# Loading q and k by eights of heads, 14 tokens to a partition

## Chip, cores and metric

One core of one Trainium2 chip. The time is the device time of one execution in microseconds (us). A ratio is the mean time of one kernel's fast runs over the mean of the other's fast runs of the same rounds, so it is not quite the ratio of the medians quoted beside it.

## The reference

Attention with normalized q and k over (8 batches, 12 heads, 448 tokens, 64 features), then a soft mixture of experts over the 3584 tokens with their 768 features.

```python
q_n, k_n = rmsnorm(q, g_q), rmsnorm(k, g_k)               # over the 64 features
attn = softmax(q_n @ k_n^T / 8);  x = attn @ v             # -> x (3584, 768)
logits = x @ phi                                          # (3584, 32), 8 experts x 4 slots
slot_input = softmax(logits, axis=0).T @ x                # (32, 768)
slot_out[e] = relu(slot_input[e] @ w1[e]) @ w2[e]         # w1 (768, 1024), w2 (1024, 768)
out = softmax(logits, axis=1) @ slot_out
```

q, k and v are 11 MB each in float32; the weights are 50 MB, stored in SBUF as bf16.

## The kernel before

It works through 24 groups of four heads (a "Q"). ACT or POOL squares the raw q and k, DVE sums, ACT makes the inverse root, POOL scales to bf16, PE transposes, DVE evacuates; then PE makes scores, ACT exponentials, PE the products with v. (PE is the matrix engine TensorE, ACT the scalar, DVE the vector and POOL the general-purpose engine.) The engine SP issues the loads of q, k and v and the stores; POOL issues the weights, one by one, after the Qs listed in `WQ`. All loads of q and k go through one function, those of v through another:

```python
def load(Q, t):                                # one transfer, 128 partitions x 2 runs of 1792 bytes
    src = (q, k)[t][Q // QB, Q % QB * 4:Q % QB * 4 + 4].rearrange("h t d -> (h t) d")
    nc.sync.dma_start(out=raw(Q, t), in_=src.rearrange("(r p s) d -> p r (s d)", r=2, s=NT))

def loadv(Q):                                  # four transfers into 64 partitions, runs of 1024 or 768 bytes
    for r in range(2):
        src = v[...].rearrange("h (p s) d -> p h (s d)", s=NT)
        m = (4 - r) * D
        nc.sync.dma_start(out=vraw(Q)[0:64, :, 4 * D * r:4 * D * r + m], in_=src[:, :, :m])
        nc.sync.dma_start(out=vraw(Q)[64:128, :, 3 * D * r:3 * D * r + NT * D - m], in_=src[:, :, m:])
# ... cut ...
WQ = [0, 2, 4, 7, 9, 12, 14, 16, 18, 20, 21, 21, 22, NQ, NQ]     # after which Q each weight is issued
```

So SP issues 2 + 4 transfers per Q, 12 per eight heads. The built program gives these transfers eight completion semaphores in turn: the trace shows eight numbers on SP's 161 transfers. From the ninth on, 150 of 153 raise the same semaphore as the eighth before them; none of the 153 is issued before that one has landed, and 34 are issued within 0.1 us of its landing.

The softmax here doesn't subtract the row's maximum and nothing guards it: scores larger than these inputs give would overflow.

Of the kernel before, what the change touches and what calls it, by code (L numbers as in the profile page):

```python
# [18 lines left out]
def kernel(  # L19
# [14 lines left out]
    assert (B, H, S, D) == (8, 12, 448, 64)  # L34
    NT = 7
# [10 lines left out]
    NPRE = 10  # L46
# [18 lines left out]
    def place(name, elems, n):  # L65
        off = sum(sizes)
        sizes.append(elems * n)
        places[name] = (off, elems, n)

    place("rawq", 2 * 2 * NT * D, 4)  # L70
    place("rawk", 2 * 2 * NT * D, 3)
    place("sq", 2 * 2 * 2 * NT * D, 1)
    place("qkn", 2 * NT * 128, 1)
    place("vraw", 2 * 2 * NT * D, 2)
    place("vext", 2 * 8 * (D + 1), 2)
    place("kT", 2 * S, 2)
    place("qT", 2 * S, 2)
    place("x", 4 * 4 * D, 4)
    place("xT", DC * 128, 4)
    place("attn", 2 * S, 7)  # L80
    arena = big.tile([128, sum(sizes)], BF16, tag="arena", name="arena")

    def at(name, i):
        off, elems, n = places[name]
        off += (i % n) * elems
        return arena[:, off:off + elems]
# [10 lines left out]
    wplace += [arena[:, i * WSZ:(i + 1) * WSZ] for i in range(4)]  # L97
    wplace += [arena[:, sum(sizes) - WSZ:], wplace[0]]
# [6 lines left out]
    def raw(Q, t):  # L105
        return at(("rawq", "rawk")[t], Q).bitcast(F32).rearrange("p (r x) -> p r x", r=2)

    def load(Q, t):
        src = (q, k)[t][Q // QB, Q % QB * 4:Q % QB * 4 + 4].rearrange("h t d -> (h t) d")
        nc.sync.dma_start(out=raw(Q, t), in_=src.rearrange("(r p s) d -> p r (s d)", r=2, s=NT))  # L110

    def vraw(Q):
        return at("vraw", Q).bitcast(F32).rearrange("p (w x) -> p w x", w=2)

    def loadv(Q):


        for r in range(2):
            src = v[Q // QB, Q % QB * 4 + 2 * r:Q % QB * 4 + 2 * r + 2].rearrange("h (p s) d -> p h (s d)", s=NT)
            m = (4 - r) * D  # L120
            nc.sync.dma_start(out=vraw(Q)[0:64, :, 4 * D * r:4 * D * r + m], in_=src[:, :, :m])
            nc.sync.dma_start(out=vraw(Q)[64:128, :, 3 * D * r:3 * D * r + NT * D - m], in_=src[:, :, m:])
# [8 lines left out]
    load(0, 0)  # L131
    load(0, 1)
# [4 lines left out]
    for Q in (1, 2):  # L137
        load(Q, 0)
        load(Q, 1)
    loadv(0)  # L140
    load(3, 0)
# [11 lines left out]
    def kT(Q):  # L153
        return at("kT", Q).rearrange("p (w c) -> p w c", w=2)

    def qT(Q):
        return at("qT", Q).rearrange("p (w c) -> p w c", w=2)
# [12 lines left out]
    def sq(t):  # L170
        return at("sq", 0).bitcast(F32).rearrange("p (t x) -> p t x", t=2)[:, t]

    def square(Q, t, pool=False):

        r = raw(Q, t).rearrange("p r x -> p (r x)")
        if pool:
            nc.gpsimd.tensor_tensor(sq(t), r, r, op=MUL)  # L177
        else:
            nc.scalar.activation(out=sq(t), in_=r, func=ACTF.Square)  # L179

    def rowsum(Q, t):

        n = Q + t
        if n not in sss:
            sss[n] = small.tile([128, 2, 2 * NT], F32, tag="ss", name="ss")
            rss[n] = small.tile([128, 2, 2 * NT], F32, tag="rs", name="rs")
        nc.vector.reduce_sum(sss[n][:, t], sq(t).rearrange("p (r d) -> p r d", d=D), axis=AX)  # L187
# [23 lines left out]
    def trans(Q, t):  # L211


        order = range(NT) if t == 0 else (0, 4, 1, 5, 2, 6, 3)
        pts[t] = psum.tile([128, NT, 128], BF16, tag="misc", name="qkTp")
        for i, s in enumerate(order):
            nc.tensor.transpose(pts[t][:, i], qkn(Q, t)[:, s], ident)  # L217

    def evac(Q, t):
        pt = pts.pop(t).rearrange("p s (w c) -> p w s c", w=2)  # L220
        if t == 0:
            nc.vector.tensor_scalar(qT(Q).rearrange("p w (s c) -> p w s c", s=NT), pt, gg, None, op0=MUL)  # L222
        else:
            nc.vector.tensor_copy(kT(Q).rearrange("p w (s c) -> p w s c", s=NT), pt)  # L224
# [31 lines left out]
    def xq(Q):  # L256
        return at("x", Q).rearrange("p (c n) -> p c n", c=4)

    def norm(Q, w, half):
        o = ovs.pop(half)[:, :, :2 * D + 2].rearrange("p c (h n) -> p c h n", h=2)  # L260
        rd = small.tile([128, 2, 2, 1], F32, tag="rd", name="rd")
        nc.vector.reciprocal(rd, o[:, :, :, D:])  # L262
        nc.vector.tensor_tensor(xq(Q).rearrange("p c (h w d) -> p c h w d", h=2, w=2)[:, 2 * half:2 * half + 2, :, w],  # L263
                                o[:, :, :, :D], rd.to_broadcast([128, 2, 2, D]), op=MUL)

    def xT(dc, n=1):
        off = places["xT"][0] + dc * 512
        return arena[:, off:off + n * 512].rearrange("p (c t) -> p c t", t=128)
# [7 lines left out]
    def moe_evac(Q):  # L276
        nc.vector.tensor_copy(xT(Q % QB * 2, 2), xps.pop(Q))  # L277
# [10 lines left out]
    def moe_sin(b):  # L288
# [17 lines left out]
        nc.vector.tensor_copy(eT[r, :, b % 2], ep[r].rearrange("n (s p) -> n s p", s=NT))  # L306


    square(0, 0)
    rowsum(0, 0)  # L310
    square(0, 1)
    rowsum(0, 1)
# [5 lines left out]
    trans(0, 1)  # L318
    square(1, 0)
# [3 lines left out]
    nc.vector.tensor_mul(gg, g2[:, 0:1], g2[:, 1:2])  # L323
    evac(0, 0)
    evac(0, 1)
    square(1, 1)
    rowsum(1, 1)
    square(2, 0)
    vcopy(0)

    WQ = [0, 2, 4, 7, 9, 12, 14, 16, 18, 20, 21, 21, 22, NQ, NQ]

    for Q in range(NQ + 2):
        on, ahead = Q < NQ, Q + 2 < NQ
        moe = Q - 2 if 0 <= Q - 2 < NQ else None
        mb = moe // QB if moe is not None and moe % QB == QB - 1 else None
        if Q == 0:
            load(4, 0)
            load(3, 1)
        elif Q + 4 < NQ:  # L340
            load(Q + 4, 1)
            if Q + 5 < NQ:
                load(Q + 5, 0)
# [3 lines left out]
        if Q == 0:  # L347
            rowsum(2, 0)
        else:
            if Q + 3 < NQ:  # L350
                square(Q + 3, 0)
            if ahead:
                square(Q + 2, 1, True)
        if 0 <= Q - 1 < NQ:
            norm(Q - 1, 0, 1)
        if Q + 1 < NQ and Q:
            for t in range(2):
                trans(Q + 1, t)
                evac(Q + 1, t)
        if ahead and Q:  # L360
            scaleqk(Q + 2, 0)
# [3 lines left out]
        if Q == 0:  # L365
            square(2, 1)
            rowsum(2, 1)
        if 0 <= Q - 1 < NQ:
            ov(Q - 1, 1, 0)
# [6 lines left out]
        if Q == 0:  # L376
            rsqrt(2)
            scaleqk(1, 1)
            trans(1, 0)
            evac(1, 0)  # L380
            scaleqk(2, 0)
            square(3, 0)
            rowsum(3, 0)
        elif Q + 3 < NQ:
            rowsum(Q + 3, 0)
# [9 lines left out]
        if ahead and Q:  # L395
            rowsum(Q + 2, 1)
        if Q == 0:
            loadv(2)
            load(5, 0)
            load(4, 1)  # L400
            loadv(3)
        elif Q + 3 < NQ:
            loadv(Q + 3)
# [3 lines left out]
        if Q == 0:  # L407
            trans(1, 1)
            evac(1, 1)
        if 0 <= Q - 1 < NQ:  # L410
            moe_x(Q - 1)
        if ahead:
            rsqrt(Q + 3, 0 if Q + 3 < NQ else 1)
            scaleqk(Q + 2, 1)
# [4 lines left out]
        if 0 <= Q - 1 < NQ:  # L419
            moe_evac(Q - 1)  # L420
        if mb is not None:
            moe_sin(mb)
# [120 lines left out]
```

## Time and profile before

| | before |
|---|---|
| time, median (range of 3 runs) | 282.89 us (282.38 to 288.27) |
| first and last attention exponential on ACT | 13.3 and 208.8 us |
| after the last exponential (experts, output) | 73.5 us |
| mean traffic of the 16 DMA engines | 247 GB/s |
| mean granted TensorE clock (share of full speed) | 0.836 |

The lines of the page, of the chain and of the DMA views are shown in the prediction. In this trace q1 has 2576 packets of 4 bytes for SP's 161 transfers, 16 each. They are read here as one completion for every DMA engine that a transfer ran on, so that the count "under 512 B" tells on how many engines the transfers ran. That is an inference; the packets in flight in the changed kernel, 4 at once for 89% of a stretch where the count says 4, agree with it (see "Which engines").

### The profile page before, as it was taken

To read this page: it belongs to the slowest core of one execution; us is meant where nothing else is said; L and a number is where in the kernel's file an instruction comes from. 1 tells how busy PE (TensorE), PEld (TensorE's weight loads), DVE (VectorE), ACT (ScalarE), POOL (GpSimd) and SP (SyncE) were. 2 spreads that over 40 slices of the span, in tenths; PEclk is the share of its full clock that TensorE was granted. 3 is DMA by queue.
4 is the path that set the end of the run, shared out by engine and by line. 5 is a ranking of instruction groups with operands and counts; after the bars stand their busy time and mean duration, and the time that the engine had idled before them with its cause. 6 is when DMAs were issued, how large, how long until landed. Compare 5 with 4: busy or idle time off the path is not lost.

```text
span 282.3 us, 8543 instructions
## 1 busy us (share of the span) xinstructions
PE 224.2 (79%) x3588; PEld 148.7 (53%) x3588; DVE 175.5 (62%) x381; ACT 191.8 (68%) x270; POOL 169.6 (60%) x189
## 2 busy tenths in 40 slices
PE   7568888998599999999989978988978655788800
PEld 3234554755365576566556545655657645743300
DVE  3756777888268889879878865866563101148800
ACT  4798999899379989998998967878850000036600
POOL 0779999994869998999999966788322000000000
PEclk9859999999789999999999995999996555555555
DMA  6999999999999999999999999969999999528997
GB/s 188 303 256 256 256 265 244 268 254 264 237 246 252 270 262 244 277 235 255 274 254 264 238 261 247 251 145 206 201 208 212 212 211 210 104 94 356 412 412 290
DMA packets 45079, 69.82 MB, mean 247 GB/s; under 512 B 3952, under 2 KB 36720, under 8 KB 45040
## 3 DMA queue, kind: packets, MB, share of 16 engines
q1 hardware_dynamic: 29328, 44.05, 53.2%
q0 software_dynamic: 15392, 25.22, 49.2%
q8 instruction: 28, 0.46, 0.6%
q14 instruction: 11, 0.09, 0.1%
q10 hardware_dynamic: 320, 0.00, 0.1%
HBM read 83.46 MB, written 11.01 MB: 335 GB/s over the span
## 4 chain that ended last, share of the span: by engine, by line
PE 31%; DMA 27%; POOL 16%; ACT 8%; issue 7%; DVE 4%; SPq 0%; POOLq 0%; ACTq 0%
DMA arena<-in_v_dram 19%; POOL arena L199 11%; DMA arena<-in_q_dram 9%; PE ov L253 6%; ACT arena L242 5%; PE sc L241 4%; PE hTp L463 4%; PE op L503 4%; PE soTp L473 4%; PE qkTp L217 3%; PE op L504 2%; POOL arena L207 2%; PE sinp L294 1%; DVE ss L187 1%; PE lg L283 1%
## 5 line engine op out<-in xcount | busy, mean ns | idle before, releaser
L242 ACT ACTIVATE arena<-sc 128x896 bf16<-128x896 f32 x168 | 144.6, 916 | 12.9 <-PE sc L241 10.1
L199 POOL TENSOR_TENSOR arena<-arena,rs 128x896 bf16<-128x896 f32 x48 | 82.2, 1715 | 17.4 <-ACT rs L192 15.9
L253 PE MATMUL ov<-arena 128*128 128x65 bf16 (+1 forms) x1344 | 64.9, 201 | 0.2 <-ACT arena L242 0.2
L253 PEld LDWEIGHTS <-arena 128*128 128x128 bf16 x1344 | 50.6, 99 | 20.0 <-issue 19.7
L241 PE MATMUL sc<-arena 64*128 64x448 bf16 x288 | 54.3, 373 | 7.4 <-ACT arena L242 6.6
L187 DVE TENSOR_REDUCE ss<-arena 128x14 f32<-128x896 f32 x48 | 51.6, 1077 | 8.4 <-ACT arena L179 8.4
L263 DVE TENSOR_TENSOR arena<-ov,rd 128x256 bf16<-128x256 f32 x96 | 40.8, 425 | 3.3
L507 ACT ACTIVATE wown<-op,arena 128x768 f32<-128x768 f32 x14 | 12.4, 900 | 42.5 <-PE op L504 42.5
L217 PE MATMUL qkTp<-ident,arena 128*128 128x128 bf16 x336 | 27.1, 226 | 16.2 <-POOL arena L199 15.5
L177 POOL TENSOR_TENSOR arena<-arena 128x896 f32<-128x896 f32 x21 | 35.4, 1688 | 0.2
L179 ACT ACTIVATE arena<-arena 128x896 f32<-128x896 f32 x27 | 25.6, 951 | 11.3 <-DMA arena<-in_q_dram 9.7
L217 PEld LDWEIGHTS <-arena 128*128 128x128 bf16 x336 | 19.7, 100 | 24.8 <-POOL arena L199 20.1
L241 PEld LDWEIGHTS <-arena 64*128 64x128 bf16 x288 | 16.6, 93 | 25.6 <-issue 13.8
L262 DVE RECIPROCAL rd<-ov 128x4 f32<-128x4 f32 x96 | 17.1, 178 | 12.9 <-PE ov L253 12.4
L224 DVE COPY arena<-qkTp 128x896 bf16<-128x896 bf16 x24 | 14.9, 622 | 11.8 <-PE qkTp L217 11.3
L222 DVE TENSOR_SCALAR arena<-qkTp,gg 128x896 bf16<-128x896 bf16 x24 | 16.4, 684 | 7.0 <-PE qkTp L217 6.7
L274 PE MATMUL xTp<-ident,arena 128*128 128x128 bf16 x192 | 18.1, 227 | 2.2 <-DVE arena L263 1.7
L277 DVE COPY arena<-xTp 128x1024 bf16<-128x1024 bf16 x24 | 16.4, 683 | 5.5 <-PE xTp L274 5.5
L207 POOL CAST arena<-arena 128x384 bf16<-128x384 f32 x24 | 12.3, 514 | 9.4 <-DMA arena<-in_v_dram 8.3
L503 PE MATMUL op<-arena,eT 32*128 32x512 bf16 x28 | 16.0, 616 | 1.4 <-ACT wown L507 0.7
L509 DVE TENSOR_SCALAR wown<-op,arena 128x768 f32<-128x768 f32 x14 | 14.2, 1017 | 4.6 <-PE op L504 4.4
L274 PEld LDWEIGHTS <-arena 128*128 128x128 bf16 x192 | 11.3, 100 | 9.9 <-DVE arena L263 5.9
(61 smaller groups left out, 204.6 us busy)
## 6 DMA issues: line engine op xcount, KB each, us to landing
wown<-in_moe_w_dram POOLq DMA_DIRECT2D x10, 1536.0 KB, 16.4
arena<-in_q_dram SPq DMA_DIRECT2D x24, 448.0 KB, 10.4
arena<-in_k_dram SPq DMA_DIRECT2D x24, 448.0 KB, 9.3
out_dram<-wown SPq DMA_DIRECT2D x11, 768.0 KB, 8.5
arena<-in_moe_w_dram POOLq DMA_DIRECT2D x5, 1536.0 KB, 19.6
arena<-in_v_dram SPq DMA_DIRECT2D x48, 128.0 KB, 8.0
arena<-in_v_dram SPq DMA_DIRECT2D x48, 96.0 KB, 8.4
out_dram<-wown SPq DMA_DIRECT2D x6, 384.0 KB, 7.1
```

The lines of the kernel that those rows point to most:

```text
L177: nc.gpsimd.tensor_tensor(sq(t), r, r, op=MUL)
L179: nc.scalar.activation(out=sq(t), in_=r, func=ACTF.Square)
L187: nc.vector.reduce_sum(sss[n][:, t], sq(t).rearrange("p (r d) -> p r d", d=D), axis=AX)
L199: (eng or nc.gpsimd).tensor_tensor(qkn(Q, t).rearrange("p s (r d) -> p s r d", r=2), raw(Q, t).rearrange("p r (s d) -> p s r d", d=D), rs. ...
L207: nc.gpsimd.tensor_copy(vext(Q)[:, :, 5:8, :D], vr[:, :, 4:7])
L217: nc.tensor.transpose(pts[t][:, i], qkn(Q, t)[:, s], ident)
L241: nc.tensor.matmul(sc[:, j, :S], kT(Q)[r, i // 4, c0:c0 + 128], qT(Q)[r, i // 4], start=True, stop=True)
L242: nc.scalar.activation(out=attn(i), in_=sc[:, :, :S], func=ACTF.Exp, scale=0.125)
L253: nc.tensor.matmul(ovs[half][:, c, o0:o0 + m], attn(i)[:, j, c0:c0 + 128], mov, start=(n == 0 and c == 0), stop=(n == 6), skip_group_check ...
L263: nc.vector.tensor_tensor(xq(Q).rearrange("p c (h w d) -> p c h w d", h=2, w=2)[:, 2 * half:2 * half + 2, :, w], o[:, :, :, :D], rd.to_bro ...
L274: nc.tensor.transpose(xps[Q][:, i], xq(Q)[:, i % 4, i // 4 * 128:i // 4 * 128 + 128], ident)
L503: nc.tensor.matmul(op[:, 0], eTtok(j, s), so4[r, :512], start=True, stop=True, tile_position=tp)
```

## The change

**Intent.** Fewer and longer packets. q and k come by eights of heads; a partition holds 14 successive tokens of a head, one run of 3584 bytes in place of two of 1792. A unit of work is then seven of the 14 tokens of all eight heads, so both units of an eight must be ready before its first Q, and everything up to the transpose moves one Q earlier. The first two Qs keep smaller loads for an early start. The larger raw buffers cost one weight its own space (nine for ten); the late weights get places that free earlier. The core of the diff:

```diff
-    NPRE = 10
+    NPRE = 9
-    def load(Q, t):
-        src = (q, k)[t][Q // QB, Q % QB * 4:Q % QB * 4 + 4].rearrange("h t d -> (h t) d")
-        nc.sync.dma_start(out=raw(Q, t), in_=src.rearrange("(r p s) d -> p r (s d)", r=2, s=NT))
+    def load(O, t):
+        src = (q, k)[t].rearrange("b h t d -> (b h) (t d)")[8 * O:8 * O + 8].rearrange("(h r) (p x) -> r h p x", r=2, p=32)
+        dst = at(("rawq", "rawk")[t], O).bitcast(F32).rearrange("p (r x) -> p r x", r=2)
+        for r in range(2):
+            nc.sync.dma_start(out=dst[:, r], in_=src[r])
+    def load4(n, t):
+        src = (q, k)[t].rearrange("b h t d -> (b h) (t d)")[4 * n:4 * n + 4].rearrange("(w r) (p a x) -> w r a p x", r=2, p=32, a=2)
+        for w in range(2):
+            for r in range(2):
+                nc.sync.dma_start(out=raw(n, t)[64 * w:64 * w + 64, r], in_=src[w, r])
     def loadv(Q):
+        src = v.rearrange("b h t d -> (b h) (t d)")[4 * Q:4 * Q + 4].rearrange("(w r) (p a x) -> r a p w x", r=2, p=32, a=2)
         for r in range(2):
-            src = v[...].rearrange("h (p s) d -> p h (s d)", s=NT)
             m = (4 - r) * D
-            (two transfers into 64 partitions)
+            for a in range(2):
+                (two transfers into 32 partitions)
-    WQ = [0, 2, 4, 7, 9, 12, 14, 16, 18, 20, 21, 21, 22, NQ, NQ]
+    WQ = [0, 2, 4, 7, 9, 11, 13, 15, 17, 18, 20, 21, 22, NQ - 1, NQ]
  ... cut: places in SBUF, evacuations by (token, half, block), the loop with units one Q earlier ...
```

More of the change, by code (lines that the diff above doesn't have):

```diff
@@ L65, in place @@
     def place(name, elems, n):
-        off = sum(sizes)
-        sizes.append(elems * n)
-        places[name] = (off, elems, n)
-    place("rawq", 2 * 2 * NT * D, 4)
-    place("rawk", 2 * 2 * NT * D, 3)
+        for _ in range(n):
+            places.setdefault(name, (elems, []))[1].append(sum(sizes))
+            sizes.append(elems)
+    for i in range(2):
+        place("rawq", 2 * 4 * NT * D, 1)
+        place("rawk", 2 * 4 * NT * D, 1)
     place("sq", 2 * 2 * 2 * NT * D, 1)
@@ L74 @@
     place("vraw", 2 * 2 * NT * D, 2)
+    for i in range(2):
+        place("kT", 4 * S, 1)
+        place("qT", 4 * S, 1)
+    place("free", 256, 1)
+    place("attn", 2 * S, 7)
     place("vext", 2 * 8 * (D + 1), 2)
-    place("kT", 2 * S, 2)
-    place("qT", 2 * S, 2)
     place("x", 4 * 4 * D, 4)
     place("xT", DC * 128, 4)
-    place("attn", 2 * S, 7)
     arena = big.tile([128, sum(sizes)], BF16, tag="arena", name="arena")
     def at(name, i):
-        off, elems, n = places[name]
-        off += (i % n) * elems
+        elems, offs = places[name]
+        off = offs[i % len(offs)]
         return arena[:, off:off + elems]
@@ L96 @@
     wplace = [wown[:, i * WSZ:(i + 1) * WSZ] for i in range(NPRE)]
-    wplace += [arena[:, i * WSZ:(i + 1) * WSZ] for i in range(4)]
-    wplace += [arena[:, sum(sizes) - WSZ:], wplace[0]]
+    wplace += [arena[:, i * WSZ:(i + 1) * WSZ] for i in range(5)]
+    o = places["attn"][1][0]
+    wplace += [arena[:, o:o + WSZ], wplace[0]]
     wview = lambda ap, i: ap.rearrange("p (c f) -> p c f", c=DC if i % 2 == 0 else FC)
@@ L103, in loadw, with raw @@
         nc.gpsimd.dma_start(out=wt[i], in_=wsrc(i))
-    def raw(Q, t):
-        return at(("rawq", "rawk")[t], Q).bitcast(F32).rearrange("p (r x) -> p r x", r=2)
-    def load(Q, t):
-        src = (q, k)[t][Q // QB, Q % QB * 4:Q % QB * 4 + 4].rearrange("h t d -> (h t) d")
-        nc.sync.dma_start(out=raw(Q, t), in_=src.rearrange("(r p s) d -> p r (s d)", r=2, s=NT))
+    def raw(n, t):
+        r = at(("rawq", "rawk")[t], n // 2).bitcast(F32)
+        if n < 2:
+            return r[:, n * 2 * NT * D:(n + 1) * 2 * NT * D].rearrange("p (r x) -> p r x", r=2)
+        return r.rearrange("p (r a x) -> p r a x", r=2, a=2)[:, :, n % 2]
+    def load(O, t):
[8 more added lines that the diff above has]
+                nc.sync.dma_start(out=raw(n, t)[64 * w:64 * w + 64, r], in_=src[w, r])
     def vraw(Q):
@@ L115, in loadv @@
     def loadv(Q):
+        src = v.rearrange("b h t d -> (b h) (t d)")[4 * Q:4 * Q + 4].rearrange("(w r) (p a x) -> r a p w x", r=2, p=32, a=2)
         for r in range(2):
-            src = v[Q // QB, Q % QB * 4 + 2 * r:Q % QB * 4 + 2 * r + 2].rearrange("h (p s) d -> p h (s d)", s=NT)
             m = (4 - r) * D
-            nc.sync.dma_start(out=vraw(Q)[0:64, :, 4 * D * r:4 * D * r + m], in_=src[:, :, :m])
-            nc.sync.dma_start(out=vraw(Q)[64:128, :, 3 * D * r:3 * D * r + NT * D - m], in_=src[:, :, m:])
+            for a in range(2):
+                nc.sync.dma_start(out=vraw(Q)[32 * a:32 * a + 32, :, 4 * D * r:4 * D * r + m], in_=src[r, a, :, :, :m])
+                nc.sync.dma_start(out=vraw(Q)[64 + 32 * a:96 + 32 * a, :, 3 * D * r:3 * D * r + NT * D - m], in_=src[r, a, :, :, m:])
     ones = const.tile([128, 128], BF16)
@@ L130 @@
         nc.tensor.matmul(warm, wone[:, :128], wone, start=True, stop=True)
-    load(0, 0)
-    load(0, 1)
+    load4(0, 0)
+    load4(0, 1)
     g2 = const.tile([128, 2], F32)
@@ L136 @@
         nc.scalar.dma_start(out=g2[half * D:(half + 1) * D, 1:2], in_=g_k.rearrange("(d o) -> d o", o=1))
-    for Q in (1, 2):
-        load(Q, 0)
-        load(Q, 1)
+    load4(1, 0)
+    load4(1, 1)
     loadv(0)
-    load(3, 0)
+    load(1, 0)
+    load(1, 1)
     loadv(1)
@@ L153, in kT @@
     def kT(Q):
-        return at("kT", Q).rearrange("p (w c) -> p w c", w=2)
+        return at("kT", Q // 2).rearrange("p (q w c) -> p q w c", q=2, w=2)[:, Q % 2]
     def qT(Q):
-        return at("qT", Q).rearrange("p (w c) -> p w c", w=2)
+        return at("qT", Q // 2).rearrange("p (q w c) -> p q w c", q=2, w=2)[:, Q % 2]
     for i in range(2):
@@ L173, in square @@
     def square(Q, t, pool=False):
-        r = raw(Q, t).rearrange("p r x -> p (r x)")
+        r, s = raw(Q, t), sq(t).rearrange("p (r x) -> p r x", r=2)
         if pool:
-            nc.gpsimd.tensor_tensor(sq(t), r, r, op=MUL)
+            nc.gpsimd.tensor_tensor(s, r, r, op=MUL)
         else:
-            nc.scalar.activation(out=sq(t), in_=r, func=ACTF.Square)
+            nc.scalar.activation(out=s, in_=r, func=ACTF.Square)
     def rowsum(Q, t):
@@ L184, in rowsum @@
         if n not in sss:
-            sss[n] = small.tile([128, 2, 2 * NT], F32, tag="ss", name="ss")
-            rss[n] = small.tile([128, 2, 2 * NT], F32, tag="rs", name="rs")
+            sss[n] = small.tile([128, 2, 2 * NT], F32, tag="ss", name="ss", bufs=3)
+            rss[n] = small.tile([128, 2, 2 * NT], F32, tag="rs", name="rs", bufs=3)
         nc.vector.reduce_sum(sss[n][:, t], sq(t).rearrange("p (r d) -> p r d", d=D), axis=AX)
@@ L219, in evac @@
     def evac(Q, t):
-        pt = pts.pop(t).rearrange("p s (w c) -> p w s c", w=2)
+        pt = pts.pop(t)
+        T = at(("qT", "kT")[t], Q // 2)
+        if Q < 2:
+            T = T.rearrange("p (q w s c) -> p q s w c", q=2, w=2, s=NT)[:, Q]
+            pt = pt.rearrange("p s (w c) -> p s w c", w=2)
+        else:
+            T = T.rearrange("p (w s a c) -> p a s w c", w=4, s=NT, a=2)[:, Q % 2]
+            pt = pt.rearrange("p s (w c) -> p s w c", w=4)
         if t == 0:
-            nc.vector.tensor_scalar(qT(Q).rearrange("p w (s c) -> p w s c", s=NT), pt, gg, None, op0=MUL)
+            nc.vector.tensor_scalar(T, pt, gg, None, op0=MUL)
         else:
-            nc.vector.tensor_copy(kT(Q).rearrange("p w (s c) -> p w s c", s=NT), pt)
+            nc.vector.tensor_copy(T, pt)
     def attn(i):
@@ L262, in norm @@
         nc.vector.reciprocal(rd, o[:, :, :, D:])
-        nc.vector.tensor_tensor(xq(Q).rearrange("p c (h w d) -> p c h w d", h=2, w=2)[:, 2 * half:2 * half + 2, :, w],
+        nc.vector.tensor_tensor(xq(Q).rearrange("p c (w h d) -> p c h w d", h=2, w=2)[:, 2 * half:2 * half + 2, :, w],
                                 o[:, :, :, :D], rd.to_broadcast([128, 2, 2, D]), op=MUL)
     def xT(dc, n=1):
-        off = places["xT"][0] + dc * 512
+        off = places["xT"][1][0] + dc * 512
         return arena[:, off:off + n * 512].rearrange("p (c t) -> p c t", t=128)
@@ L305, in moe_sin @@
                                 tile_position=(lo, b // 2 * NS))
-        nc.vector.tensor_copy(eT[r, :, b % 2], ep[r].rearrange("n (s p) -> n s p", s=NT))
-    square(0, 0)
-    rowsum(0, 0)
-    square(0, 1)
-    rowsum(0, 1)
+        nc.vector.tensor_copy(eT[r, :, b % 2].rearrange("n s (p a) -> n s a p", a=2),
+                              ep[r].rearrange("n (s a p) -> n s a p", s=NT, a=2))
+    for t in range(2):
+        square(0, t)
+        rowsum(0, t)
     rsqrt(0, 0, 1)
@@ L318 @@
     trans(0, 1)
+    nc.vector.tensor_mul(gg, g2[:, 0:1], g2[:, 1:2])
+    evac(0, 0)
+    evac(0, 1)
     square(1, 0)
@@ L322 @@
     scaleqk(1, 0)
-    nc.vector.tensor_mul(gg, g2[:, 0:1], g2[:, 1:2])
-    evac(0, 0)
-    evac(0, 1)
     square(1, 1)
     rowsum(1, 1)
+    rsqrt(2, 1, 2)
     square(2, 0)
     vcopy(0)
-    WQ = [0, 2, 4, 7, 9, 12, 14, 16, 18, 20, 21, 21, 22, NQ, NQ]
+    WQ = [0, 2, 4, 7, 9, 11, 13, 15, 17, 18, 20, 21, 22, NQ - 1, NQ]
     for Q in range(NQ + 2):
-        on, ahead = Q < NQ, Q + 2 < NQ
+        on = Q < NQ
         moe = Q - 2 if 0 <= Q - 2 < NQ else None
         mb = moe // QB if moe is not None and moe % QB == QB - 1 else None
-        if Q == 0:
-            load(4, 0)
-            load(3, 1)
-        elif Q + 4 < NQ:
-            load(Q + 4, 1)
-            if Q + 5 < NQ:
-                load(Q + 5, 0)
         if on:
@@ L347 @@
         if Q == 0:
+            scaleqk(1, 1, nc.vector)
+            load(2, 0)
+            load(2, 1)
             rowsum(2, 0)
-        else:
+            rsqrt(2, 0, 1)
+            square(2, 1, True)
+            trans(1, 0)
+            evac(1, 0)
+            scaleqk(2, 0)
+        elif Q == 1:
+            square(4, 0)
+        else:
+            if Q + 4 < NQ:
+                square(Q + 4, 0)
             if Q + 3 < NQ:
-                square(Q + 3, 0)
-            if ahead:
-                square(Q + 2, 1, True)
+                square(Q + 3, 1, True)
         if 0 <= Q - 1 < NQ:
             norm(Q - 1, 0, 1)
-        if Q + 1 < NQ and Q:
+        if Q + 2 < NQ and Q:
             for t in range(2):
-                trans(Q + 1, t)
-                evac(Q + 1, t)
-        if ahead and Q:
-            scaleqk(Q + 2, 0)
+                trans(Q + 2 if Q > 1 else 2, t)
+                evac(Q + 2 if Q > 1 else 2, t)
+        if Q == 1:
+            scaleqk(3, 0)
+        elif Q + 3 < NQ and Q > 1:
+            scaleqk(Q + 3, 0)
+            if Q % 2 == 0 and Q + 6 < NQ:
+                load(Q // 2 + 3, 0)
         if on:
@@ L365 @@
         if Q == 0:
-            square(2, 1)
             rowsum(2, 1)
+            square(3, 0)
+        elif Q == 1:
+            scaleqk(3, 1, nc.vector)
+            load(3, 0)
+            load(3, 1)
+            square(4, 1, True)
         if 0 <= Q - 1 < NQ:
@@ L376 @@
         if Q == 0:
-            rsqrt(2)
-            scaleqk(1, 1)
-            trans(1, 0)
-            evac(1, 0)
-            scaleqk(2, 0)
-            square(3, 0)
-            rowsum(3, 0)
-        elif Q + 3 < NQ:
-            rowsum(Q + 3, 0)
+            rsqrt(3, 1, 2)
+            trans(1, 1)
+            evac(1, 1)
+            scaleqk(2, 1)
+            rowsum(3, 0)
+            square(3, 1, True)
+        elif Q == 1:
+            rowsum(4, 0)
+            trans(3, 0)
+            evac(3, 0)
+            rsqrt(4, 0, 1)
+            scaleqk(4, 0)
+        elif Q + 4 < NQ:
+            rowsum(Q + 4, 0)
         if on:
@@ L394 @@
             norm(Q - 1, 1, 1)
-        if ahead and Q:
-            rowsum(Q + 2, 1)
         if Q == 0:
+            rowsum(3, 1)
             loadv(2)
-            load(5, 0)
-            load(4, 1)
-            loadv(3)
         elif Q + 3 < NQ:
+            rowsum(Q + 3, 1)
+        if Q + 3 < NQ:
             loadv(Q + 3)
@@ L406 @@
             score(Q, 4)
-        if Q == 0:
-            trans(1, 1)
-            evac(1, 1)
+        if Q == 1:
+            trans(3, 1)
+            evac(3, 1)
         if 0 <= Q - 1 < NQ:
             moe_x(Q - 1)
-        if ahead:
-            rsqrt(Q + 3, 0 if Q + 3 < NQ else 1)
-            scaleqk(Q + 2, 1)
+        if Q == 0:
+            rsqrt(3, 0, 1)
+            rsqrt(4, 1, 2)
+        elif Q + 3 < NQ:
+            if Q == 1:
+                rsqrt(5, 1, 2)
+                square(5, 0)
+            else:
+                rsqrt(Q + 4, 0 if Q + 4 < NQ else 1)
+            scaleqk(Q + 3, 1)
+            if Q % 2 == 0 and Q + 6 < NQ:
+                load(Q // 2 + 3, 1)
         if on:
@@ L420 @@
             moe_evac(Q - 1)
+        if Q == 1:
+            rowsum(5, 0)
+            rsqrt(5, 0, 1)
         if mb is not None:
```

## The prediction

In this text and in the expectations, k is the number of DMA engines that one transfer runs on, and a ring is the work that is queued for one engine. That k would be 4 for the loads of eight heads and 2 for load4, and that the same few engines would serve them all, no trace showed when this was written: it was the author's estimate, and the result tests it. The estimate of 393 us for the last k is the 383 of the sum plus 10 for empty stretches between loads, about 1 us for an eight, which no trace showed either.

> **What bounds the kernel now.** I read the page first (engines, slices, DMA queues), then the chain that ended last in order of time, then the DMA view over two stretches, then what the DMA-issuing queue (SP) waits for. From the page:
>
> ```profile
> span 282.3 us, 8543 instructions
> ...
> DMA  6999999999999999999999999969999999528997
> ...
> DMA packets 45079, 69.82 MB, mean 247 GB/s; under 512 B 3952, under 2 KB 36720, under 8 KB 45040
> ...
> q1 hardware_dynamic: 29328, 44.05, 53.2%
> q0 software_dynamic: 15392, 25.22, 49.2%
> ```
>
> The DMA row is 9 in nearly every slice. No compute engine is above 80% (PE 79%, ACT 68%). q1 is what SP issues (q, k, v and the output), q0 the weights, cast on the way. Together they are 102% of the 16 engines' span. But a full row alone doesn't prove that DMA sets the time, since weights can wait. The chain tells more:
>
> ```profile
> 26.87 1.72 POOL arena L199
> ...
> 34.61 1.72 POOL arena L199
> ...
> 42.39 1.71 POOL arena L199
> ...
> 46.16 12.04 DMA arena<-in_v_dram
> 58.29 12.45 DMA arena<-in_v_dram
> ...
> 145.37 13.85 DMA arena<-in_q_dram
> 159.23 9.74 DMA arena<-in_v_dram
> ...
> 172.34 12.00 DMA arena<-in_v_dram
> ```
>
> L199 is the scaling of q and k on POOL, twice per four heads (a "Q"); the listed ones are 7.75 us apart, which is the compute pace of one Q. Over 60 us of the chain are transfers that landed late. Yet 24 Qs at 7.75 us are 186 us, and the last attention exponential in this chain (ACT L242 at 207.90 for 0.94 us) ends at 209 us after a head of about 13 us (its first L242 is at 13.31 in the time line of ACT). So late transfers really cost some 10 us; the rest of those 60 us passes beside compute. The tail from 209 to 282 us (73 us) is the expert layers and the output.
>
> Two stretches where q1 works almost alone give the cost of a packet: 8 to 16 us (loads of 768, 1024 and 1792 bytes), then 256 to 280 us (output of 3072 and 6144 bytes).
>
> ```profile
> DMA packets 1895, 2.31 MB, mean 289 GB/s; under 512 B 220, under 2 KB 1895, under 8 KB 1895
> ...
> q1 hardware_dynamic: 1829, 2.31, 108.7%
> ```
> ```profile
> DMA packets 2074, 9.87 MB, mean 411 GB/s; under 512 B 225, under 2 KB 225, under 8 KB 2073
> ...
> q1 hardware_dynamic: 2073, 9.87, 101.5%
> ```
>
> The first: 1.087 x 16 engines x 8 us / 1829 = 76 ns for a mean of 1263 bytes. The second: 1.015 x 16 x 24 us / 2073 = 188 ns for 4761. So about 0.032 ns a byte and 35 ns a packet, or 150 ns for 3584 bytes. The trace's packet records by single size (1792 bytes 95 ns in the first 8 us, 1024 bytes 65 to 75 ns) give nearer 165 ns; I take 160. A full engine shows about 1.10 of packet time per microsecond because packets overlap.
>
> [...]under 512 B there are 3952 packets, and 161 SP transfers x 16 completion packets = 2576, 18 of POOL x 16 = 288, four gain loads of 64 rows and 16 completions = 320, and 768 pieces of phi make exactly that. It shows no k below 16.[...]
>
> **The change, part by part.**
>
> *Removed.* q and k came as 128 partitions x 2 runs of 1792 bytes: 12288 packets x 95 ns / 16 = 73 us of all engines. From the second eight heads on, runs are 3584 bytes: 5632 x 160 / 16 = 56 us, plus 1024 old ones, 6 us. So 11 us of full DMA time would be saved, if all 16 engines did it.
>
> *Added, and the point on which all hangs.* In the built program the load of eight heads has 4 x 32 x 896 as source and 128 x 1 x 896 as destination, because the heads of one parity do not lie behind one another.[...] The load of the first fours (load4) has 2 x 32 x 448 into 64 partitions: k is 2. The v loads are 32 x 2 on both sides: k stays 16, with 8 transfers per Q in place of 4. So all q and k pass through four engines.
>
> *Compute.* PE has 7178 rows of instructions in both programs; squares, sums, scalings, evacuations keep number and size, shifted one Q earlier in the pipeline. Two scalings move from POOL (1.7 us each) to DVE in the head. About 0 us.
>
> *Weights.* One weight less has its own space; one-and-a-half later ones wait for freed space. They are prefetched far ahead if attention gets longer. About 0.
>
> *Sum, head.* [...]16 transfers x 32 packets x 95 / 1.09 = 45 us before anything else; ACT stands in order at the square of the third unit, which needs the second eight heads (64 packets x 160 / 1.09 = 9 us more). First exponential near 58 us, not 13.
>
> *Sum, steady.* For eight heads (two Qs) [...]q and k 2 x 256 rows / 4 = 128 packets x 160 = 20.5 us; v 64 x 60 = 3.8 us; its sixteenth of the weights: q0 is 0.492 x 282.3 = 139 us per engine for 16 weights, 8.7 each, 13 of them in 11 eights: 10.3 us. Together 34.6 / 1.10 = 31.5 us, against 15.5 us of compute. The loads are issued about one such period ahead (two buffers)[...]. The second eights, without weights, end at 46 + 22 = 68 us; ten more at 31.5 end at 383. SP has eight completion semaphores, and each transfer waits for the eighth before it:
>
> ```profile
> SPq L121 <- POOL arena L209: 51.8, 19, 5.0
> SPq L121 <- DMA arena<-in_k_dram: 15.1, 13, 3.1
> SPq L122 <- DMA arena<-in_q_dram: 10.8, 7, 2.3
> ```
>
> (the lower two lines are such waits). With 8 v transfers between a q and a k load that window is used up by v[...]. The last k is used four Qs later: + 31 = 424 us at the end of attention. The tail is 73 us now; about 10 us of it are waits for weights, which mostly landed earlier then: + 63. Sum **487 us**.
>
> **The rivals.** (a) *All 16 engines work after all* (something below the program merges or splits the pattern). Then 11 us of DMA time go, of which the 10 us of late transfers are the most that can come back; the first loads become small, and twice as many v transfers share eight semaphores: 270 to 282 us, most likely 275. For it: a tuned schedule like this is rarely written for nothing.[...] (b) *k is 4, but the four engines are chosen in turn.* Then the load evens out and only the latency of one transfer grows (32 packets x 160 = 5 us, twice): 280 to 300 us.[...] (c) *Four engines, but faster alone:* at the 26 GB/s per engine that the output reaches (411 / 16), 128 packets are 17.9 us and not 18.6 after overlap: only 7 us less in all, 480. (d) *DMA hidden anyway*, compute the bound: a full fourfold concentration can't hide, as 20.5 us of q and k alone exceed the 15.5 us of compute.
>
> **Range and chances.** I give 84% to few and fixed engines, 16% to (a) or (b). In the first, the size is uncertain by the packet's cost (140 to 175 ns: 27 to 34 us per eights, +-35 us), by idle rings and by the tail: 415 to 550 holds it. (a) and (b) lie outside the range, so it holds about 8 times in 10. Faster 0.11, within 2% 0.05, slower 0.84.
>
> **What would show it.** Packets under 512 B count completions: 16 x 2 + 44 x 4 + 192 x 16 + 17 x 16 = 3552, and 1376 from the other queues: 4928 if k is 2 and 4; 5680 if all are 16. Mean GB/s should fall to about 145, and the DMA row to digits 4 to 6 in attention, never 9; ACT's waits for in_q should rise from 10 us to well over 100; q and k transfers should land in over 15 us (now 10.4 and 9.3); the granted clock should rise. The chain should be in_q and in_k transfers. I am wrong if the DMA row stays at 9, and the q loads land in under 10 us.

## The result, and the profile after

The changed kernel took **500.38 us** in the median (499.04 to 500.76, 4 runs), against 283.14; ratio 1.768, 95% interval 1.762 to 1.774. The prediction was 487 with a range of 415 to 550.

The page of the changed kernel:

```profile
span 499.0 us, 8677 instructions
...
PEclk9555558566769577795695676775956689955555
DMA  1122328234838333836628338356384939997398
...
DMA packets 40424, 69.83 MB, mean 140 GB/s; under 512 B 4928, under 2 KB 26432, under 8 KB 40384
...
q0 software_dynamic: 15392, 25.22, 28.9%
q1 hardware_dynamic: 24672, 44.05, 26.9%
```

The same bytes move at 140 GB/s, not 247. The DMA row is 1 to 3 at first, then swings between 2 and 8: from 199 to 206 us, as a weight comes in, the engines' share is 1.10 and the traffic 212 GB/s; from 190 to 198 us, without one, 0.38 and 96 GB/s. Packets under 512 B are 4928, exactly the count worked out for k = 2 and 4; for 16 engines everywhere it was worked out to 5680, which e5 later showed.

What the engines wait for (us in total, times, longest), and the chain in order of time (start, length, what):

```profile
ACT arena L202 <- DMA arena<-in_q_dram: 95.6, 10, 13.4
...
POOL arena L200 <- DMA arena<-in_k_dram: 72.2, 8, 21.0
...
POOL arena L229 <- DMA arena<-in_v_dram: 64.5, 9, 10.7
```
```profile
190.66 1.69 POOL arena L200
192.63 16.05 DMA arena<-in_v_dram
208.69 14.92 DMA arena<-in_k_dram
223.77 1.69 POOL arena L200
225.75 17.40 DMA arena<-in_v_dram
243.16 14.33 DMA arena<-in_k_dram
257.64 1.69 POOL arena L200
```

L200 is the square of k on POOL, here the first one after each wait for an eight's k. From 190.66 over 223.77 to 257.64, and on to 291.61 and 324.57 in the same view, eight heads (one "eight" from here on) take 33.5 us; compute would need 15.5. Nearly all of it is waiting for loads (from 190.66 to 223.77 us the chain has 16.05 for v and 14.92 for k). (v is named too: SP issues eight v loads between the q of an eight at 190.93 us and its k at 207.97.) The first exponential is at 58.2 us, the last ends at 428.0; 71 us follow.

### The profile page after: what moved, and what is told of

Its sections match the earlier page's. It is cut to its first block, busy times and chain, and to the rows that moved or that the text cites. A ratio compares the mean times of both kernels' runs of the same rounds, so it can differ in the third digit from the quotient of the medians.

```text
span 499.0 us, 8677 instructions
## 1 busy us (share of the span) xinstructions
PE 260.1 (52%) x3588; PEld 169.9 (34%) x3588; DVE 183.6 (37%) x383; ACT 195.7 (39%) x277; POOL 166.5 (33%) x188
## 2 busy tenths in 40 slices
DMA packets 40424, 69.83 MB, mean 140 GB/s; under 512 B 4928, under 2 KB 26432, under 8 KB 40384
## 4 chain that ended last, share of the span: by engine, by line
DMA 71%; PE 11%; SPq 5%; issue 3%; POOL 3%; ACT 3%; DVE 2%; POOLq 0%; ACTq 0%
DMA arena<-in_k_dram 32%; DMA arena<-in_v_dram 27%; DMA arena<-in_q_dram 12%; SPq L132 3%; PE hTp L520 2%; PE op L560 2%; PE soTp L530 2%; ACT arena L271 2%; POOL arena L200 2%; SPq L125 1%; PE op L561 1%; PE ov L282 1%; POOL arena L222 1%; PE sc L270 1%; DVE ss L210 0%
## 5 line engine op out<-in xcount | busy, mean ns | idle before, releaser
L271 ACT ACTIVATE arena<-sc 128x896 bf16<-128x896 f32 x168 | 146.4, 914 | 31.9 <-PE sc L270 26.5
L270 PE MATMUL sc<-arena 64*128 64x448 bf16 x288 | 65.0, 446 | 77.6 <-ACT arena L271 76.7
L222 POOL TENSOR_TENSOR arena<-arena,rs 128x896 bf16<-128x896 f32 x46 | 78.8, 1713 | 50.7 <-ACT rs L215 40.3
L282 PE MATMUL ov<-arena 128*128 128x65 bf16 (+1 forms) x1344 | 76.9, 218 | 0.2 <-ACT arena L271 0.2
L282 PEld LDWEIGHTS <-arena 128*128 128x128 bf16 x1344 | 61.1, 110 | 26.8 <-issue 26.5
L200 POOL TENSOR_TENSOR arena<-arena 128x896 f32<-128x896 f32 x22 | 37.0, 1683 | 98.6 <-DMA arena<-in_k_dram 72.2
L239 PE MATMUL qkTp<-ident,arena 128*128 128x128 bf16 x336 | 35.8, 272 | 48.4 <-POOL arena L222 48.3
L266 PE MATMUL sc<-arena 64*64 64x448 bf16 x96 | 17.9, 454 | 70.4 <-ACT arena L271 70.4
L239 PEld LDWEIGHTS <-arena 128*128 128x128 bf16 x336 | 26.5, 122 | 59.2 <-POOL arena L222 53.4
L229 POOL CAST arena<-arena 128x384 bf16<-128x384 f32 x24 | 12.1, 505 | 79.8 <-DMA arena<-in_v_dram 64.5
L214 ACT ACTIVATE ss<-ss,eps 128x28 f32<-128x28 f32 (+1 forms) x30 | 9.3, 312 | 66.0 <-DVE ss L210 66.0
L266 PEld LDWEIGHTS <-arena 64*64 64x64 bf16 x96 | 5.3, 116 | 71.7 <-issue 70.1
L253 DVE COPY arena<-qkTp 128x896 bf16<-128x896 bf16 x24 | 14.9, 622 | 26.2 <-PE qkTp L239 26.0
L230 POOL CAST arena<-arena 128x384 bf16<-128x384 f32 x24 | 12.3, 514 | 24.1 <-DMA arena<-in_v_dram 21.5
```

What stands on the lines that cost most here:

```text
L200: nc.gpsimd.tensor_tensor(s, r, r, op=MUL)
L222: (eng or nc.gpsimd).tensor_tensor(qkn(Q, t).rearrange("p s (r d) -> p s r d", r=2), raw(Q, t).rearrange("p r (s d) -> p s r d", d=D), rs. ...
L239: nc.tensor.transpose(pts[t][:, i], qkn(Q, t)[:, s], ident)
L266: nc.tensor.matmul(sc[r, j, :S], kT(Q)[r, j, 384:], qT(Q)[r, j], start=True, stop=True, tile_position=(64 * hh, 64 * hh))
L270: nc.tensor.matmul(sc[:, j, :S], kT(Q)[r, i // 4, c0:c0 + 128], qT(Q)[r, i // 4], start=True, stop=True)
L271: nc.scalar.activation(out=attn(i), in_=sc[:, :, :S], func=ACTF.Exp, scale=0.125)
```

## Experiments

All kernels below gave correct results. "Packet records" are the times of single DMA packets in the traces. First and last exponential are read from ACT's instructions in each trace:

| kernel | time, us (median) | first exp | last exp | after it |
|---|---|---|---|---|
| before | 283 to 284 | 13.3 | 208.8 | 73.5 |
| changed | 500.4 | 58.2 | 428.0 | 71.0 |
| e1_all16 | 325.3 | 20.1 | 254.0 | 70.7 |
| e2_oct_k2 | 710.8 | 65.1 | 641.0 | 70.4 |
| e3_first16 | 471.1 | 26.3 | 398.3 | 71.0 |
| e4_eights16 | 355.3 | 50.7 | 282.8 | 70.6 |
| e5_ports16 | 304.6 | 18.6 | 230.5 | 71.4 |
| e6_v64 | 284.2 | 18.7 | 212.9 | 70.1 |
| e7a_head | 283.2 | 14.7 | 208.5 | 70.6 |
| e7_head_wq (3 of 6 runs slow; mean of the fast ones 288.8) | 291.2 | 14.6 | 216.4 | 70.1 |
| b1_v8 | 308.6 | 13.3 | 234.1 | 72.5 |
| b2_qk64 | 296.7 | 14.9 | 222.3 | 72.2 |
| b3_qk128x2 | 289.8 | 13.2 | 215.0 | 73.9 |
| b4_wq | 288.3 | 12.8 | 213.0 | 72.9 |

### e1_all16: all loads of q and k on all engines

Undoes nothing of the change but the shape of the loads: cut along the heads, so that the slowest dimension is 32 on both sides. Places, packets and schedule stay.

```diff
-  ...rearrange("(h r) (p x) -> r h p x", r=2, p=32)
-  for r in range(2):
-      nc.sync.dma_start(out=dst[:, r], in_=src[r])
+  ...rearrange("(h r) (p x) -> h p r x", r=2, p=32)
+  for h in range(4):
+      nc.sync.dma_start(out=dst[32 * h:32 * h + 32], in_=src[h])
   # load4 likewise: "-> w a p r x", transfers into 32 partitions
```

> All q and k loads of the changed kernel cut along the heads (32 partitions, both rows of a partition in one transfer) so that the slowest dimension is 32 on both sides; same places, same 3584-byte and 1792-byte packets, everything else unchanged. Transfers per eight heads rise from 20 to 24. Theory (k = 4 and 2 concentrates q and k on a few engines): the concentration is gone, 270 to 290 us, first attention exponential near 15 to 20 us, 6384 packets under 512 B (16 completions for each of 313 SP transfers, and 1376). Rival A (the eight completion semaphores, used up by many small transfers, starve the rings): it gets no better, 500 us or more. Rival B (the long packets or the later pipeline are slow by themselves): about 500 us.

Measured: 325.34 us (324.92 to 326.49), ratio to before 1.146; 6384 packets under 512 B, as counted. So 175 of the 217 us are gone, and both rivals fail as explanations of the 500 us: more transfers were issued than in the changed kernel, and the packets were as long. But it stays 42 us above the kernel before and 35 above what was expected, which the later runs follow up.

### e2_oct_k2: k = 2

```diff
+  for g in range(2):
+      nc.sync.dma_start(out=dst[64 * g:64 * g + 64, r], in_=src[r][2 * g:2 * g + 2])    # source 2 x 32 x 896
```

> The loads of eight heads cut into halves of 64 partitions with a source of 2 x 32 x 896, so that k should be 2; transfers per eight heads rise from 20 to 24 as in e1. Theory: [...]256 packets x 165 ns + 3.8 + 10.3 us per eight heads, 56 / 1.1 = 51 us in place of 31.5, so with ten and a half eights about 200 us more: 680 to 730 us. Rival A (number of transfers in the window): 500 to 560 us. If the engines were chosen in turn[...]: about 500 us or less.

Measured: 710.77 us (one round). The chain of this kernel:

```profile
314.34 20.67 DMA arena<-in_k_dram
337.13 27.74 DMA arena<-in_q_dram
366.99 19.88 DMA arena<-in_k_dram
388.98 28.19 DMA arena<-in_q_dram
419.82 19.58 DMA arena<-in_k_dram
```

The waits for k loads begin 52.7 us apart (314.34 to 366.99 to 419.82), for an estimate of 51. Halving the engines from four to two costs what the sum of packets says. With engines chosen in turn, about 500 us or less were expected. e1 and e2 issue the same number of transfers and move the same packets; they are 385 us apart.

### e3_first16 and e4_eights16: head and steady part

e3 takes only the new load4 of e1, e4 only its new load.

> Only the loads of the first two fours of heads are put on all 16 engines; the eights stay at k = 4. Theory: [...]the first exponential comes near 20 us and not at 58, and the end comes 30 to 42 us earlier: 458 to 470 us; the pace of an eight stays 33.5 us. Rival: if the head were hidden[...], about 500 us.

> Only the loads of eight heads are put on all 16 engines; the first two fours stay at k = 2. Theory: the head stays long (first exponential near 50 us, as the second eight now needs 3 us and not 9), the rest runs at 7.75 us per four heads: 305 to 325 us. Head and steady part should add up: what e3 and e4 save together is what e1 saves, within 10 us.

Measured: 471.07 and 355.31 us. Against the changed kernel, e3 saves 29.3 us and e4 145.1, together 174.4; e1 saves 175.0. So the two terms add up, as expected. Their sizes were a little off: e3 missed its range by 1 us (first exponential at 26, not 20), and e4 by 30, because it shares with e1 the unexplained 40 us.

### e5_ports16: whole transfers of 128 partitions

What is left in e1? Every q and k load of e1 goes into 32 partitions, and there are 24 transfers per eight heads. Theory P is that the packets of a transfer are slower when it covers half of the 128 partitions or fewer; theory W, that the number of transfers costs the time. e5 puts the blocks of tokens outside and the heads inside: source 32 x 4 x 896, destination 128 partitions, k still 16.

```diff
-  ...rearrange("(h r) (p x) -> r h p x", r=2, p=32)
+  ...rearrange("(h r) (p x) -> r p h x", r=2, p=32)
+  identp: the identity with its columns in the order of heads, for the transposes of the eights
```

> e1 ended at 325 us, 40 us above the kernel before, with 3584-byte packets at 216 to 260 ns. The loads of eight heads are now one transfer per row over all 128 partitions, in the order block of tokens by head (source 32 x 4 x 896, so k should be 16); the transpose uses a permuted identity to give the same columns; the first fours as in e1; v as in the changed kernel. 20 transfers per eight heads as in the changed kernel. Theory P[...]: packets fall to 150 to 180 ns, and the time to 280 to 295 us. Theory W (too many transfers for eight completion semaphores and for SP): only four transfers fewer per eights, so 310 to 322 us, and SP still waits most for the eighth transfer before.

Measured: 304.62 us (303.05 to 306.64), 20.7 less than e1. Between the two theories' ranges: neither is the whole. The DMA queue lines over 40 us of each (packets, MB, share), first e1 from 120 to 160 us, then e5 from 100 to 140 us:

```profile
q1 hardware_dynamic: 3802, 5.40, 53.0%
```
```profile
q1 hardware_dynamic: 3749, 5.54, 44.7%
```

q1 took 9.8% of the engines' time per MB in e1, and 8.1% in e5. In the packet records of these stretches a 3584-byte packet took 216 ns in e1 and 166 in e5. e5 also has 20 transfers per eight heads and e1 24, so how the 20.7 us split between the two causes is not told by this pair.

### e6_v64: v in four transfers again

```diff
-  src = ...rearrange("(w r) (p a x) -> r a p w x", r=2, p=32, a=2)     # 8 transfers of 32 partitions
+  src = ...rearrange("(w r) (p x) -> r p w x", r=2, p=64)              # 4 transfers of 64 partitions
-  k: T.rearrange("p (w s a c) -> p a s w c", ...)
+  k: T.rearrange("p (w s c a) -> p a s w c", ...)                      # evacuation writes every second element
   # load4 of k likewise in two transfers of 64 partitions, in place of four of 32
```

> e5, and v in four transfers of 64 partitions per four heads as in the kernel before (the keys then stand in the order token, block, half; the evacuation of k writes with a stride of two elements[...]); 12 transfers per eight heads, as before. Theory W: most of what is left of the 40 us goes here, 270 to 285 us. Theory P: at most a few us against e5.

Measured: 284.19 us (282.67 to 285.0), ratio to before 1.004 (0.998 to 1.010). Another 20.4 us, and the kernel is where it started. The q and k packets are 3584 bytes here as the change intended, 12 transfers per eight heads, all on 16 engines.

### b1_v8: only more transfers, in the kernel before

```diff
+  for a in (0, 32):   # each v transfer of 64 partitions cut in two of 32
```

> The kernel before, with its v loads cut in halves of 32 partitions: 20 transfers per eight heads in place of 12, the same bytes and packets, and nothing else. Theory W: 295 to 320 us. Theory P: v went into 64 partitions of one half before and into 32 now[...]: 281 to 288 us, within 2%.

Measured: 308.64 us, ratio 1.091 (1.083 to 1.098). Eight more transfers per eight heads cost 25.5 us, with the same bytes in the same packets. The DMA row of this kernel, from 100 to 140 us, the same stretch of the kernel before, and what SP waits for in b1:

```profile
DMA  9999973849999999999930699991489983799999
```
```profile
DMA  9999999999999999999999999999999999999999
```
```profile
SPq L122 <- DMA arena<-in_k_dram: 33.1, 11, 4.6
SPq L123 <- DMA arena<-in_q_dram: 29.3, 20, 4.2
```

The row of b1 has holes where that of the kernel before has none: SP stands at a v load (L122, L123) until an earlier q or k load has landed, though the engines are running dry. No v load reads or overwrites anything of q or k; the only tie is the eighth semaphore back: in b1's trace 148 of the 192 v loads wait for the very semaphore that they will raise, in the kernel before 52 of 96. Eight v loads are now of 48 and 64 KB and not of 96 and 128, so such a window of eight holds half the bytes; the mean traffic is 228 GB/s, for 247 in the kernel before. Two rivals fail by the same trace. The packets were not slower (those of 1792 bytes took 88 ns in the mean, for 98 in the kernel before; those of v, into 32 partitions, 47 and 59, for 54 and 66 into 64). And SP issues a load in some 0.4 us when it doesn't wait, so 20 of them fill 8 of the 18 us that an eight takes here. (A program with more semaphores was not run.)

### b2_qk64 and b3_qk128x2: which partitions one transfer covers

Both cut each q and k load of the kernel before in two, so both have 16 transfers per eight heads. b2 cuts by partitions, b3 by runs.

```diff
   src = src.rearrange("(r p s) d -> p r (s d)", r=2, s=NT)
+  for a in (0, 64): nc.sync.dma_start(out=raw(Q, t)[a:a + 64], in_=src[a:a + 64])    # b2
+  for a in range(2): nc.sync.dma_start(out=raw(Q, t)[:, a], in_=src[:, a])           # b3
```

> The kernel before, with its q and k loads cut in two transfers of 64 partitions each: 16 transfers per eight heads, packets of 1792 bytes as before. Theory P: the packets of q and k go from 97 to some 120 ns or more and the time to 295 to 315 us. Theory W: half the added transfers of b1, so half of its loss.

> The control of b2: the kernel before, with its q and k loads cut in two transfers again, but each over all 128 partitions (one of the two 1792-byte rows of a partition in each). 16 transfers per eight heads as in b2; only the partitions that one transfer covers differ. b2 took 297 us with packets of q and k at 104 to 123 ns, against 97 in the kernel before. Theory P (a transfer that covers part of the partitions has slower packets): packets back at 90 to 100 ns and 282 to 288 us. Theory W (the number of transfers alone): 293 to 299 us as b2.

Measured: b2 296.70, b3 289.84 us (ratios 1.050, 1.045 to 1.054, and 1.022, 1.014 to 1.030, in different batches). From 100 to 140 us, the DMA row and q1's line of b2, then of b3:

```profile
DMA  9999999999999999999999999999999999999999
...
q1 hardware_dynamic: 5328, 6.21, 66.8%
```
```profile
DMA  9999999999999999978787988698999999999999
...
q1 hardware_dynamic: 5354, 6.47, 57.3%
```

b2's engines are full and do less: 10.8% of their time per MB, against 8.9% in b3; its 1792-byte packets took 104 to 123 ns in the packet records, b3's 93 to 98. So both theories hold and can be told apart: four more transfers cost about 6 us (b3), and half the partitions another 7 to 8 (b2). b3 fell just between its two ranges for that reason. (One more thing differs and was not separated: a transfer of b2 reads two pieces of 112 KB of a tensor, one of b3 a single piece of 224 KB.)

### e7a_head, e7_head_wq, b4_wq: can the longer packets be made to pay?

e7a gives e6 the head of the kernel before; e7_head_wq also issues the first nine weights one place earlier; b4 does that to the kernel before.

```diff
-  gg; evac(0, 0); evac(0, 1); square(1, 0); ...; rsqrt(2, 1, 2); square(2, 0)
+  square(1, 0); rowsum(1, 0); rsqrt(1, 0, 1); scaleqk(1, 0); gg; evac(0, 0); evac(0, 1); ...   # e7a
-  WQ = [0, 2, 4, 7, 9, 11, 13, 15, 17, 18, ...]
+  WQ = [0, 0, 2, 4, 7, 9, 11, 13, 15, 18, ...]                                                # e7_head_wq
-  WQ = [0, 2, 4, 7, 9, 12, 14, 16, 18, 20, ...]
+  WQ = [0, 0, 2, 4, 7, 9, 12, 14, 16, 18, ...]                                                # b4_wq
```

> e6 (284 us, first attention exponential at 18.7 us against 13.3 in the kernel before) with the head put back in the order of the kernel before: the second unit of q squared, summed and scaled before the first evacuations, and the third unit squared after the first scores. If the late start is what e6 loses: first exponential at 14 to 15 us and 279 to 282 us. If the end is set by the weights alone (DMA full from 185 to 236 us in e6): no change, 283 to 285 us.

> e7a, and the first nine weights each issued one place earlier (two after the first four heads), so that the thin stretch of DMA from 20 to 40 us of e6 (0.88 of 16 engines) is filled and one weight less is left for the end. If the end is set by the total of DMA: 5 to 8 us less than e7a, 272 to 277 us, the first to beat the kernel before by over 2%. If the early weights only delay the loads of q and k: 280 us or more.

> The control of e7_head_wq: the kernel before with its own first ten weights one place earlier. Its DMA row is full already from 7 us on, so nothing should be gained: 280 to 286 us. If it gains as much as e7_head_wq does, the order of the weights is an improvement by itself and owes nothing to the longer packets.

Measured: 283.22, 291.22 and 288.27 us, ratios 0.998 (0.992 to 1.004), 1.019 (1.011 to 1.026) and 1.021 (1.014 to 1.028). e7a starts 4 us earlier than e6 and gains 1 us in the median, no more than the spread of its fast runs (281.08 to 284.34). Earlier weights lose in both kernels, about 6 us each (fast runs: 288.8 against 282.9 for e7a, 1.021 times the kernel before for b4): the idea that they would fill a thin stretch and shorten the end was wrong. Part of the reason is seen below: the long pauses of PE at the end are not waits for weights. No version of this layout beat the kernel before by 2%.

## Why the prediction was right, and where it was not

**Which engines.** Right, and the step that carried everything, though no trace showed it beforehand. With 2 completions for each load whose slowest dimension was 2, 4 for 4, and 16 for 32, 64 and 128, the counts under 512 B of seven kernels come out exactly: 3952 before, 4928 changed, 6384 in e1, 5680 in e5, 4080 in e6, 5488 in b1, 4720 in b2. That different transfers share the same engines is seen in the packet records of the changed kernel. Four loads of the second eight (two of q, two of k) are issued from 42.8 to 47.1 us, and their packets run until 65.8. With engines taking turns, up to 16 would have had such packets at once; but between 48 and 57 us the 3584-byte packets in flight were 4 for 89% of the time and never more than 6. In the stretch where the first loads run on two engines it is 2, and in e2 it is 2 as well; in e1 and e5 it reaches 16 and more. (Which engines they are, the trace doesn't number.)

**Head.** First exponential near 58 us; it was 58.2. The exact hit is luck, as two misses cancel. The first loads were in at 42 us and not at 46, because their packets took 80 ns in the records and not 95; and from there to the square of the third unit (57.4 us) it was 15 us and not 9: SP issued the first load of the second eight only at 42.8 us, and the wait of that square ended at 57.4. Put on 16 engines alone (e3), the head gives back 29 us.

**Steady part.** 31.5 us and a bubble of about 1 us for an eight; it was 33.5. The term slightly too small is the packet: 160 ns was assumed, the records of the changed kernel show 168 in the mean (157 to 180 over stretches of 34 us). From 190 to 390 us at least four packets, of all queues, were in flight for 93% of the time, and packets of 3584 bytes for 75%; that fits four engines which stay nearly full, though the trace does not number them. One sum of the prediction is wrong: packets of 140 to 175 ns make 29 to 33 us per eight, not 27 to 34, so the +-35 us drawn from it should have been about 20.

**End of attention.** 424 us; it was 428. Here too the parts are further off than the sum. The last packet of k landed at 391 us for an estimate of 393, since the first eights came at 27 to 36 us each; from there it took 37 us and not 31.

**The rest of the time.** "The tail is 73 us now; about 10 us of it are waits for weights, which mostly landed earlier then: + 63." This failed: 71.0 us. What was wrong is the reading of the pauses: they are not waits for weights. The chain shows the same ones between matmuls of the experts, in the kernel before and in the changed one (start, length; "issue" is time in which PE waited for nothing that the profile shows):

```profile
225.34 2.37 issue
...
231.26 2.37 issue
```
```profile
444.38 2.37 issue
...
450.31 2.37 issue
```

By the packet records, the weights of the matmuls on both sides of these pauses had landed by 153 and 170 us in the kernel before, and by 315 and 349 us in the changed one. The pauses come after the 3039th and the 3167th matmul in both programs, in the middle of a layer, and each begins within 0.2 us of a packet of 16 KB on the queue that the page calls "instruction" (q8). What PE waits for there, no run tested. In all kernels 70 to 74 us follow the last exponential, however long attention takes.

These 8 us and the 4 of attention are the whole difference between 487 and 499.

**The gain that all 16 engines would have had.** "11 us of full DMA time would be saved", and rival (a) at 270 to 282 us. e6, where the long packets do run on all engines with as few transfers as before, is at 284, so that gain was not seen. The packet is one reason: 3584 bytes took 175 ns in e6 in the mean (165 to 189), where two packets of 1792 took 2 x 98 = 195 in the kernel before. So the q and k packets of e6 cost 68 us of all engines for 75, a saving of 7 and not 11. Why even these 7 don't show in the time stays open. It isn't the late start of e6: e7a takes 4 of the 5 us back and gains 1. e6, which writes k with a step of two elements, also evacuates it in 1128 ns in the mean and not in 622. Rival (a) also took the eight additional v transfers for a small matter; b1 shows 25 us for them, and e5, which is what rival (a) describes, took 305 us and not 275.

**Signs.** The count of completions was exact. The mean traffic was near (140 GB/s for 145). The DMA row was not a steady 4 to 6 but swung from 2 to 8. ACT's waits for q were 96 us and not well over 100, beside 72 us of POOL for k and 65 for v. In the chain, k had 32%, v 27% and q 12%; the share of v was not foreseen. The granted clock did not rise: 0.668 for 0.836. PE was busy for 52% of the span, for 79% before; the PEclk row of the changed kernel (shown above) stands mostly at 5 to 7 through attention, where that of before (below) has mostly 9. Why, no run tested. The landing times could not be read, as the profile gave none for SP's transfers in the changed kernel.

```profile
PEclk9859999999789999999999995999996555555555
```

**The whole account of the 217 us**, from the runs: few engines 196 (changed to e5, which has the same 20 transfers per eight heads, the same packets, and loads of the eights over the same 128 partitions), eight small v transfers per eight heads 20 (e5 to e6), and a rest of 1. e1 showed only 175 of the 196, because its own cut brought a new cost: loads into 32 partitions, and four more transfers per eight heads (21 us, e1 to e5).

## What to carry to other kernels

Before you trust a longer run in a DMA, write down the slowest dimension of source and destination as the built program has it: here the loads that began with 4 heads, with 32 x 896 inside, ran on 4 engines, and the number of 4-byte completion packets in the profile (4928 under 512 B, for 5680 in e5) showed it at a glance. Compare a transfer over part of the partitions with one over all 128 (64 cost b2 7 to 8 us against b3), and keep transfers few; put the small dimension inside (32 x 4 in e5, which had 16 engines, not 4 x 32) and let a permuted identity in the transpose restore the order (a transpose took 241 ns with it in e5, and 242 without in e1). When a split is forced, count the transfers against the window of completion semaphores before you count bytes: with eight of them, eight more v transfers per eight heads cost b1 25.5 us with no byte added. And take a packet's time from the stretch in question: 1792 bytes took 80 ns in the head of the changed kernel, 98 in the kernel before, and 104 to 123 in b2.
